# Reading the moving operand's columns alternately from its two halves in both products of a feed-forward stage

## The chip, the core and the metric

The kernel runs on one core of a Trainium2 chip. The metric is device time in microseconds (us), the median over several executions. One further execution was recorded by the hardware profiler; every row quoted below is from that one.

## The reference: what is computed

```python
def _attn_ref(q, k, v, alpha):                # B, H, S, D = 4, 8, 768, 48
    state = np.zeros((B, H, D, D))
    for t in range(S):
        state = alpha[:, :, t, :, None] * state + np.einsum('bhd,bhe->bhde', k[:, :, t], v[:, :, t])
        y[:, :, t] = np.einsum('bhd,bhde->bhe', q[:, :, t], state)

def _moe_ref(x, w_in, w_out):                 # x: 3072 x 384, w_in: 384 x 2048, w_out: 2048 x 384
    h = x @ w_in
    g = np.where(h > 0.0, h, np.exp(np.minimum(h, 0.0)) - 1.0)
    return g @ w_out
```

A gated linear attention over 4 batches, 8 heads and 768 positions gives 3072 rows of 384 numbers. A feed-forward stage (FFN) with an ELU between its two products turns these into the output of 3072 x 384.

## The kernel before, in words

**Attention.** The sequence is cut into 24 windows of 128 positions (6 per batch). A window's operands are loaded on SyncE's queue. VectorE (DVE in the rows) scans the decays, ScalarE (ACT) takes logarithm and exponential, VectorE and GpSimd (POOL) scale keys and queries. TensorE (PE) makes scores (lines L337, L353), state updates (L381, L399) and outputs (L460, L465) by small matmuls. The result of two windows becomes one block `xt` of 256 tokens, held with the 384 features on the partitions, as a rounded part and a rest.

**FFN.** Everything there is done in a split form: each operand is a rounded part of the type float32r plus a rest of the same type, and three of the four cross products are added up. There are 12 blocks of 256 tokens and, for each, 8 steps `j` over 256 of the 2048 hidden units.

- `A(b, j)`, line L662: the first product. The weights are stationary (128 x 128) and the tokens move: each matmul reads 256 columns (tokens) of `xt`. Nine matmuls for each of two groups of 128 hidden units, 18 in all, write one tile `h` (128 x 2 x 256) in PSUM. Over the kernel that is 12 x 8 x 18 = 1728 matmuls.
- `RA`, `RB` on ScalarE, `RC` on VectorE: the ELU. `GH` on ScalarE and `GL` on VectorE make `gh` and `gl`, the rounded part and the rest.
- `O(b, j)`, line L713: the second product. Here `gh` or `gl` (128 hidden units x 128 tokens) is stationary and the weights move: each matmul reads 384 columns of a `w` tile. For each of two halves `m` of the tokens there are six matmuls into an accumulator `o` of 128 x 384 in PSUM; 12 x 8 x 12 = 1152 matmuls in all.
- `Z(b)`: ScalarE copies the two accumulators out and a DMA writes 128 output rows each.

All moving operands of these two products are read column after column from one contiguous run of 4-byte elements: 256 tokens (1 KB in each partition) and 384 weights (1.5 KB).

**Order.** The order in which the work stands on each engine is written out by hand: the string `START` up to the fourth block, and then the string `STEADY`, repeated for each further block with shifts. Each entry is one of the steps above with a window, or a block and a step. The tile framework adds the semaphores. Pools rotate: `gh` and `gl` have three buffers each, `xt` two, and PSUM eight banks, all in one pool.

**Start.** After 12 bfloat16 matmuls on a constant that keep TensorE busy, a helper `probe` (L134) issues further matmuls on a constant tile `fr` (128 x 512, float32r), whose results nobody reads: in this order 5 and 4 of 256 contiguous columns, 8 in bfloat16 of 256 columns (on the same constant as the first 12), 4 whose moving operand is one column of `fr` broadcast to 256, 4 of 256 columns on 64 partitions, and 3 of 512 columns. They stand on TensorE ahead of the first window's transposes (L289).

**Another path.** A function `general` holds a slower version for operands out of the usual range; it is behind a flag and is not executed with these inputs.

Of the kernel before, what the change touches and what calls it, by code (L numbers as in the profile page):

```python
# [14 lines left out]
B, H, S, D = 4, 8, 768, 48  # L15
# [5 lines left out]
DM, DF = 384, 2048  # L21
NC = DM // 128
BLK = 256
NBLK = B * S // BLK
NJ = DF // 256
# [63 lines left out]
def gla_elu_ffn(ctx: ExitStack, tc: tile.TileContext, qka, vv, vn, wgt, out):  # L89
    nc = tc.nc  # L90
# [15 lines left out]
    for a in range(2):  # L106
        nc.vector.tensor_copy(out=sel[64 * a:64 * a + 64, a, :, D:64],
                              in_=ident[64 * a:64 * a + 64, 64 * a:64 * a + D].rearrange("p (x c) -> p c x", c=NC))
# [4 lines left out]
    for h0 in (0, 64):  # L113

        nc.gpsimd.affine_select(
            out=mask[h0:h0 + 64, :], in_=mask[h0:h0 + 64, :], pattern=[[1, C]],
# [5 lines left out]
    wz = first.rearrange("p n w -> p (n w)").bitcast(mybir.dt.bfloat16)  # L122
# [6 lines left out]
    fr = const.tile([128, 512], F32R, name="fr")  # L129
    nc.scalar.copy(out=fr, in_=first.rearrange("p n w -> p (n w)")[:, 0:512])  # L130

    def probe(n, w, lhs, rhs, start):
        for _ in range(n):
            nc.tensor.matmul(wp[:, 0:w], lhsT=lhs, rhs=rhs, start=start, stop=True, skip_group_check=True)  # L134

    probe(5, 256, fr[:, 0:128], fr[:, 0:256], True)
    probe(4, 256, fr[:, 0:128], fr[:, 0:256], False)
    probe(4, 256, wz[:, 0:128], wz[:, 0:256], False)
    probe(4, 256, wz[:, 0:128], wz[:, 0:256], True)
    probe(4, 256, fr[:, 0:128], fr[:, 0:1].broadcast_to([128, 256]), False)  # L140
    probe(4, 256, fr[0:64, 0:128], fr[0:64, 0:256], False)
    probe(3, 512, fr[:, 0:128], fr[:, 0:512], False)

    NB = 4

# [411 lines left out]
    raw, wm, wl, ck, wt, spare = {}, {}, {}, {}, {}, []  # L557
# [93 lines left out]
    @tok  # L651
    def A(b, j):
        x = xt[b]
        h = psa.tile([128, 2, BLK], F32, name="h", tag="pa")
        ff[b, j] = dict(h=h)
        for f in range(2):
            k = 0
            t = wgts[2 * j]
            for c in range(NC):
                ws = slice(f * DM + c * 128, f * DM + c * 128 + 128)  # L660
                for wi, xi in ((0, 0), (0, 1), (1, 0)):
                    nc.tensor.matmul(h[:, f, :], lhsT=t[:, wi, ws], rhs=x[:, c, xi, :],  # L662
                                     start=(f == 0 and k == 0), stop=(k == 8), skip_group_check=True)
                    k += 1

# [35 lines left out]
    @tok  # L701
    def O(b, j):
        d = ff.pop((b, j))
        gh, gl = d["gh"], d["gl"]
        if j == 0:
            ops_[b] = [psa.tile([128, 512], F32, name="o", tag="pa") for _ in range(2)]
        for m in range(2):
            o = ops_[b][m]
            ms = slice(m * 128, m * 128 + 128)
            for f in range(2):  # L710
                t = wgts[2 * j + 1]
                for k, (gt, wi) in enumerate(((gh, 0), (gh, 1), (gl, 0))):
                    nc.tensor.matmul(o[:, 0:DM], lhsT=gt[:, f, ms], rhs=t[:, wi, f * DM:f * DM + DM],  # L713
                                     start=(j == 0 and f == 0 and k == 0),
                                     stop=(j == NJ - 1 and f == 1 and k == 2))

# [46 lines left out]
    with tc.manual_schedule():  # L763
        for name, *at in steady():
            TOK[name](*at)
    main.close()
    general(ctx, tc, ident, [t[:, 0] for t in wgts], [t[:, 1] for t in wgts], flag[0], qka, vn, wgt, out)


# [26 lines left out]
def general(ctx, tc, ident, whi, wlo, flag, qka, vn, wgt, out):  # L796

    nc = tc.nc
    WCH = 2 * DM
    good = nc.values_load(flag[0:1, 0:1], min_val=0, max_val=1)  # L800
    with tc.If(good < 1):
        with ExitStack() as st:
# [5 lines left out]
            for f in range(2 * NJ):  # L808
# [4 lines left out]
                m = sb.tile([128, WCH], F32, name="gwm", tag="gwm")  # L813
# [24 lines left out]
            with tc.For_i(0, B) as b:  # L838
                with tc.For_i(0, NP) as n:
# [7 lines left out]
                    for a in range(2):  # L847
                        nc.sync.dma_start(out=vp[:, :, a, 0:D],
                                          in_=vn4[bass.ds(b, 1), :, :, bass.ds(n * 2 + a, 1), :]
# [7 lines left out]
                    for e in range(D):  # L857
# [3 lines left out]
                        for x in range(2):  # L861
                            nc.tensor.matmul(vb[:, x, 0:HS], lhsT=bc.rearrange("p a x -> p (a x)"),
                                             rhs=vt[:, x * HS:(x + 1) * HS], start=True, stop=True)
# [7 lines left out]
                        for x in range(2):  # L871
                            nc.tensor.matmul(yp[:, x, 0:HS], lhsT=pick[:, 64 - e:192 - e],
                                             rhs=sc[:, x * HS:(x + 1) * HS], start=(e == 0), stop=(e == D - 1))
                    ys = sb.tile([128, S], F32, name="gys")
                    nc.vector.tensor_copy(out=ys.rearrange("p (x t) -> p x t", x=2), in_=yp[:, :, 0:HS])
                    nc.sync.dma_start(out=yd[bass.ds(b, 1), bass.ds(n, 1)].rearrange("b n p s -> (b n p) s"), in_=ys)

            with tc.For_i(0, B) as b:
                with tc.For_i(0, S // BLK) as t:
                    xf = sb.tile([128, NC, BLK], F32, name="gxf")  # L880
                    for a in range(2):
                        for c in range(NC):
                            nc.sync.dma_start(
                                out=xf[64 * a:64 * a + D, c],
                                in_=yd[bass.ds(b, 1), c, 64 * a:64 * a + D, bass.ds(t * BLK, BLK)]
                                .rearrange("b p s -> (b p) s"))
                            nc.sync.dma_start(
                                out=xf[64 * a + D:64 * a + 64, c],
                                in_=yd[bass.ds(b, 1), NP - 1, 64 * a:64 * a + D, bass.ds(t * BLK, BLK)]
                                .rearrange("b (p c) s -> c (b p) s", c=NC)[c])  # L890
                    xh = sb.tile([128, NC, BLK], F32R, name="gxh")
                    xl = sb.tile([128, NC, BLK], F32R, name="gxl")
                    nc.vector.tensor_copy(out=xh, in_=xf)
                    nc.vector.tensor_tensor(out=xl, in0=xf, in1=xh.bitcast(F32), op=ALU.subtract)
                    op = [ps.tile([128, 512], F32, name=f"go{m}", tag=f"go{m}") for m in range(2)]
                    for f in range(2 * NJ):
                        h = ps.tile([128, BLK], F32, name="gh")
                        k = 0
                        fi, fo, f0 = f - f % 2, f - f % 2 + 1, f % 2 * DM
                        for c in range(NC):  # L900
                            ws = slice(f0 + c * 128, f0 + c * 128 + 128)
                            for wt, xt in ((whi[fi], xh), (whi[fi], xl), (wlo[fi], xh)):
                                nc.tensor.matmul(h, lhsT=wt[:, ws], rhs=xt[:, c], start=(k == 0), stop=(k == 8))
                                k += 1
                        r = sb.tile([128, BLK], F32, name="gr", tag="gr", bufs=2)
                        nc.scalar.activation(out=r, in_=h, func=AF.Relu, scale=-1.0)
                        nc.scalar.activation(out=r, in_=r, func=AF.Exp, scale=-1.0)
                        nc.vector.scalar_tensor_tensor(out=r, in0=r, scalar=-1.0, in1=h, op0=ALU.add, op1=ALU.max)
                        gh = sb.tile([128, BLK], F32R, name="ggh", tag="ggh", bufs=2)
                        gl = sb.tile([128, BLK], F32R, name="ggl", tag="ggl", bufs=2)  # L910
                        nc.vector.tensor_copy(out=gh, in_=r)
                        nc.vector.tensor_tensor(out=gl, in0=r, in1=gh.bitcast(F32), op=ALU.subtract)
                        ws = slice(f0, f0 + DM)
                        for m in range(2):
                            ms = slice(m * 128, m * 128 + 128)
                            for k, (gt, wt) in enumerate(((gh, whi[fo]), (gh, wlo[fo]), (gl, whi[fo]))):
                                nc.tensor.matmul(op[m][:, 0:DM], lhsT=gt[:, ms], rhs=wt[:, ws],
                                                 start=(f == 0 and k == 0), stop=(f == 2 * NJ - 1 and k == 2))
                    for m in range(2):
                        ot = sb.tile([128, DM], F32, name="got", tag="got", bufs=2)  # L920
                        nc.scalar.copy(out=ot, in_=op[m][:, 0:DM])
                        nc.sync.dma_start(out=out[bass.ds(b * S + t * BLK + m * 128, 128), :], in_=ot)


# [50 lines left out]
```

## Time and profile before

| | |
|---|---|
| median of 3 executions | 508.41 us (507.92 to 510.58) |
| the profiled execution's own time | 507.37 us |
| its span, first to last instruction | 505.7 us |
| TensorE busy (matmuls) | 495.8 us, 98% |
| TensorE weight loads busy | 480.1 us, 95% |
| VectorE busy | 391.2 us, 77% |
| ScalarE busy | 289.6 us, 57% |
| GpSimd busy | 129.2 us, 26% |
| mean granted TensorE clock | 0.998 of full speed |

The first figure to read is TensorE's busy share, and then the chain of waits, which says whether TensorE's work is what the end waited for. A caution on the duration of a matmul: a matmul of 256 columns lasts 282 ns by its row, but the next one starts long before it ends. What a matmul costs in a dense stretch is the distance from one start to the next; a row of the chain that merges many matmuls gives it, as its time divided by its count.

### The profile page before, as it was taken

Reading aid. Unit: us, or ns where it says so; the run is one execution under the profiler, and the core shown is the slowest. Engines: PE = TensorE matmul, PEld = TensorE weight load, DVE = VectorE, ACT = ScalarE, POOL = GpSimd, SP = SyncE. Lnnn points to the kernel's source line nnn. Section 1 sums busy time; section 2 is a strip of 40 time slices with the busy share of each in tenths; the row PEclk is TensorE's granted clock in tenths of the full one; section 3 lists DMA queues with packets and bytes.
Section 4 is the critical chain, followed back from the end, with each engine's and each line's share of the span. In section 5 each row is a group of like instructions: output and inputs, shape, how many; then the busy total and the mean of one; then the engine's idle time right before and its main releaser. Section 6 shows DMA issues by size and latency. Waiting matters only on the chain.

```text
span 505.7 us, 13302 instructions
## 1 busy us (share of the span) xinstructions
PE 495.8 (98%) x5428; PEld 480.1 (95%) x5428; DVE 391.2 (77%) x808; ACT 289.6 (57%) x690; POOL 129.2 (26%) x108
## 2 busy tenths in 40 slices
PE   8899999998999999999999999999999999999996
PEld 5689999998999999999999999999999999999996
DVE  7999999998899679769969969778978987344221
ACT  3655875744652666647755755646755755454432
POOL 2024954633321301501501501501501500000000
PEclk9999999999999999999999999999999999999999
DMA  8997615034503135235235234234333321110001
GB/s 304 416 412 308 190 48 203 1 94 145 143 1 126 35 108 199 55 109 186 67 110 168 85 110 166 85 109 162 95 102 103 95 72 41 62 40 10 2 32 37
DMA packets 22404, 61.15 MB, mean 121 GB/s; under 512 B 2880, under 2 KB 9792, under 8 KB 22336
## 3 DMA queue, kind: packets, MB, share of 16 engines
q1 hardware_dynamic: 22048, 59.83, 35.3%
q8 instruction: 45, 0.74, 0.6%
q10 hardware_dynamic: 288, 0.39, 0.2%
q14 instruction: 23, 0.19, 0.1%
HBM read 53.53 MB, written 4.72 MB: 115 GB/s over the span
## 4 chain that ended last, share of the span: by engine, by line
PE 93%; DVE 2%; DMA 2%; ACT 1%; SPq 1%; issue 0%; DVEq 0%
PE h L662 41%; PE o L713 40%; PE y L465 4%; PE y L460 2%; PE q L381 2%; PE q L337 2%; DMA qka<-in_qka_dram 1%; PE sc L353 1%; PE u L399 1%; DMA xt<-y 1%; PE y L504 1%; DVE wm L594 0%; DVE wm L600 0%; PE tp L289 0%; DVE qka L238 0%
## 5 line engine op out<-in xcount | busy, mean ns | idle before, releaser
L662 PE MATMUL h<-xt,w 128*128 128x256 f32 x1728 | 215.5, 282 | 1.3 <-DMA xt<-y 1.3
L662 PEld LDWEIGHTS h<-xt,w 128*128 128x128 f32 x1728 | 209.6, 188 | 3.3 <-issue 1.6
L713 PE MATMUL o<-w,gh 128*128 128x384 f32 x768 | 199.1, 340 | 0.0
L713 PEld LDWEIGHTS o<-w,gh 128*128 128x128 f32 x768 | 136.9, 188 | 0.8
L713 PE MATMUL o<-w,gl 128*128 128x384 f32 x384 | 129.9, 338 | 0.0
L686 ACT CAST gh<-h 128x512 fp32r<-128x512 f32 x96 | 56.1, 584 | 80.7 <-DVE h L680 41.4
L699 DVE TENSOR_TENSOR gl<-h,gh 128x512 fp32r<-128x512 f32 x96 | 65.9, 687 | 36.5 <-ACT gh L686 35.0
L299 DVE STREAM_TRANSPOSE kn<-qka 32x128 f32<-32x128 f32 x288 | 87.2, 303 | 4.5
L670 ACT ACTIVATE r<-h 128x512 f32<-128x512 f32 x96 | 57.0, 597 | 52.9 <-PE h L662 50.8
L680 DVE SCALAR_TENSOR_TENSOR h<-r,h 128x512 f32<-128x512 f32 x96 | 64.4, 689 | 16.2 <-ACT r L675 15.3
L238 POOL TENSOR_TENSOR qka<-qka,R 128x512 f32<-128x512 f32 x19 | 25.3, 1334 | 189.1 <-DVE gl L699 117.0
L713 PEld LDWEIGHTS o<-w,gl 128*128 128x128 f32 x384 | 72.1, 188 | 0.0
L675 ACT ACTIVATE r<-r 128x512 f32<-128x512 f32 x96 | 59.1, 632 | 0.6
L268 POOL TENSOR_TENSOR st<-qka,P 64x512 f32<-64x512 f32 x36 | 43.6, 1212 | 15.1 <-DVE P L216 13.3
L365 DVE TENSOR_TENSOR st<-q,mask 64x256 f32<-64x256 f32 x72 | 30.4, 422 | 10.8 <-ACT vs L416 9.2
L216 DVE TENSOR_TENSOR_SCAN P<-qka,first 128x516 f32<-128x516 f32 x24 | 30.2, 1263 | 1.6 <-DMA qka<-in_qka_dram 0.8
L243 POOL TENSOR_TENSOR R<-P,R 128x512 f32<-128x512 f32 x20 | 25.9, 1297 | 7.3 <-DVE qka L238 5.9
L225 ACT ACTIVATE R<-P 128x512 f32<-128x512 f32 x24 | 15.2, 634 | 20.7 <-DVE P L216 20.7
L418 DVE TENSOR_TENSOR vs<-vs,q 48x192 f32<-48x192 f32 x30 | 10.5, 349 | 19.1 <-PE q L337 16.9
L518 ACT ACTIVATE y<-y 128x128 fp32r<-128x128 f32 x20 | 5.6, 278 | 29.7 <-PE y L465 27.4
L618 ACT ACTIVATE ck<-ck,lim 128x384 f32<-128x384 f32 x32 | 20.7, 648 | 0.1
L646 POOL TENSOR_TENSOR w<-spare,w 128x768 fp32r<-128x768 f32 x6 | 15.8, 2649 | 18.8 <-DMA vs<-in_vv_dram 13.0
(106 smaller groups left out, 433.8 us busy)
## 6 DMA issues: line engine op xcount, KB each, us to landing
qka<-in_qka_dram SPq DMA_DIRECT2D x22, 770.0 KB, 6.6
raw<-in_wgt_dram SPq DMA_DIRECT2D x16, 768.0 KB, 10.1
ck<-in_wgt_dram SPq DMA_DIRECT2D x32, 384.0 KB, 3.2
vs<-in_vv_dram SPq DMA_DIRECT2D x36, 192.0 KB, 3.8
out_dram<-ot SPq DMA_DIRECT2D x22, 192.0 KB, 2.0
vs<-in_vv_dram SPq DMA_DIRECT2D x6, 384.0 KB, 10.0
xt<-y SPq DMA_DIRECT2D x40, 48.0 KB, 2.3
qka<-in_qka_dram SPq DMA_DIRECT2D x2, 512.0 KB, 6.1
```

Of the source, the lines that this page charges most:

```text
L216: nc.vector.tensor_tensor_scan(out=P.rearrange("p n w -> p (n w)"), data0=t[:, 2 * NP * W:], data1=first.rearrange("p n w -> p (n w)"), in ...
L243: eng(KBV, i).tensor_tensor(out=d["R"], in0=pw(i), in1=d["R"], op=ALU.mult)
L268: eng(SQV, i).tensor_tensor(out=st[r, a], in0=d["q"][r], in1=pw(i)[r], op=ALU.mult)
L299: nc.vector.transpose(out=kn[32 * t:32 * t + 32, :, 32 * g:32 * g + 32], in_=d["kt"][32 * g:32 * g + 32, :, 32 * t:32 * t + 32])
L365: nc.vector.tensor_tensor(out=d["st"][r, a, :, c * C:(c + 1) * C], in0=d["s4"][a][o], in1=mask[o].unsqueeze(1).broadcast_to([64, NP, C]), ...
L662: nc.tensor.matmul(h[:, f, :], lhsT=t[:, wi, ws], rhs=x[:, c, xi, :], start=(f == 0 and k == 0), stop=(k == 8), skip_group_check=True)
L670: nc.scalar.activation(out=r, in_=d["h"], func=AF.Relu, scale=-1.0)
L675: nc.scalar.activation(out=d["r"], in_=d["r"], func=AF.Exp, scale=-1.0)
L680: nc.vector.scalar_tensor_tensor(out=d["h"], in0=d["r"], scalar=-1.0, in1=d["h"], op0=ALU.add, op1=ALU.max)
L686: nc.scalar.copy(out=gh, in_=d["h"])
L699: nc.vector.tensor_tensor(out=gl, in0=d["h"], in1=d["gh"].bitcast(F32), op=ALU.subtract)
L713: nc.tensor.matmul(o[:, 0:DM], lhsT=gt[:, f, ms], rhs=t[:, wi, f * DM:f * DM + DM], start=(j == 0 and f == 0 and k == 0), stop=(j == NJ - ...
```

## The change

Both products keep their numbers of matmuls and their operands; the order in which the moving columns are read is another. In `A`, the 256 tokens are read as token 0, token 128, token 1, token 129, and so on: the access pattern has an inner dimension of 2 with a step of 128 elements (512 bytes) and an outer one of 128 with a step of 1. So the columns of `h`, `gh` and `gl` hold the tokens in that order, and the output rows come out in it; the host puts the rows back. In `O`, the 384 weights are read as column 0, column 192, column 1, and so on (inner step 768 bytes). The host lays out w_out's columns with the even ones in the first half and the odd ones in the second, so that `o` comes out in the natural order. The path `general` gets the same two forms.

The probes at the start are others: 14 matmuls in place of 28, all float32r on `fr`, all read in such alternating forms: 512 and 384 columns from two halves (3 each), 256 columns from four quarters (3) and from eight parts (2), and 512 columns from four quarters (3).

Apart from the probes, the instructions on each engine stand in the same order as before.

```diff
-    probe(5, 256, fr[:, 0:128], fr[:, 0:256], True)
-    probe(4, 256, fr[:, 0:128], fr[:, 0:256], False)
-    probe(4, 256, wz[:, 0:128], wz[:, 0:256], False)
-    probe(4, 256, wz[:, 0:128], wz[:, 0:256], True)
-    probe(4, 256, fr[:, 0:128], fr[:, 0:1].broadcast_to([128, 256]), False)
-    probe(4, 256, fr[0:64, 0:128], fr[0:64, 0:256], False)
-    probe(3, 512, fr[:, 0:128], fr[:, 0:512], False)
+    def cols(n, k):
+        return fr[:, 0:n].rearrange("p (a x) -> p x a", a=k)
+
+    for n, k in ((512, 2), (384, 2), (256, 4), (256, 8), (512, 4)):
+        probe(3 if k < 8 else 2, n, fr[:, 0:128], cols(n, k), True)
...
-                    nc.tensor.matmul(h[:, f, :], lhsT=t[:, wi, ws], rhs=x[:, c, xi, :],
+                    nc.tensor.matmul(h[:, f, :], lhsT=t[:, wi, ws], rhs=x[:, c, xi, :].rearrange("p (a x) -> p x a", a=2),
                                      start=(f == 0 and k == 0), stop=(k == 8), skip_group_check=True)
...
-                    nc.tensor.matmul(o[:, 0:DM], lhsT=gt[:, f, ms], rhs=t[:, wi, f * DM:f * DM + DM],
+                    nc.tensor.matmul(o[:, 0:DM], lhsT=gt[:, f, ms],
+                                     rhs=t[:, wi, f * DM:f * DM + DM].rearrange("p (a x) -> p x a", a=2),
                                      start=(j == 0 and f == 0 and k == 0),
                                      stop=(j == NJ - 1 and f == 1 and k == 2))
...
-    wo = w_out.reshape(NJ, 2, 128, DM).transpose(0, 2, 1, 3).reshape(NJ, 128, 2 * DM)
+    cols = np.arange(DM).reshape(DM // 2, 2).T.reshape(-1)
+    wo = w_out[:, cols].reshape(NJ, 2, 128, DM).transpose(0, 2, 1, 3).reshape(NJ, 128, 2 * DM)
...
-    return r.results[0]["out_0_dram"]
+    return np.ascontiguousarray(r.results[0]["out_0_dram"].reshape(NBLK, 128, 2, DM).transpose(0, 2, 1, 3)
+                                ).reshape(B * S, DM)
```

More of the change, by code (lines that the diff above doesn't have):

```diff
@@ L876, in general @@
                     nc.sync.dma_start(out=yd[bass.ds(b, 1), bass.ds(n, 1)].rearrange("b n p s -> (b n p) s"), in_=ys)
+            out4 = out.rearrange("(t x a) d -> t x a d", a=2, x=128)
             with tc.For_i(0, B) as b:
@@ L916, in general @@
                             for k, (gt, wt) in enumerate(((gh, whi[fo]), (gh, wlo[fo]), (gl, whi[fo]))):
-                                nc.tensor.matmul(op[m][:, 0:DM], lhsT=gt[:, ms], rhs=wt[:, ws],
+                                nc.tensor.matmul(op[m][:, 0:DM], lhsT=gt[:, ms],
+                                                 rhs=wt[:, ws].rearrange("p (a x) -> p x a", a=2),
                                                  start=(f == 0 and k == 0), stop=(f == 2 * NJ - 1 and k == 2))
@@ L921, in general @@
                         nc.scalar.copy(out=ot, in_=op[m][:, 0:DM])
-                        nc.sync.dma_start(out=out[bass.ds(b * S + t * BLK + m * 128, 128), :], in_=ot)
+                        nc.sync.dma_start(out=out4[bass.ds(b * (S // BLK) + t, 1), :, m]
+                                          .rearrange("t x d -> (t x) d"), in_=ot)
 def kernel(**inputs):
```

## The prediction

> **What bounds the kernel now.** I read the page's busy shares first, then its chain of waits, and then the same chain in order of time for the blocks in the middle.
>
> ```profile
> span 505.7 us, 13302 instructions
> PE 495.8 (98%) x5428; PEld 480.1 (95%) x5428; DVE 391.2 (77%) x808; ACT 289.6 (57%) x690; POOL 129.2 (26%) x108
> PEclk9999999999999999999999999999999999999999
> ...
> PE 93%; DVE 2%; DMA 2%; ACT 1%; SPq 1%; issue 0%; DVEq 0%
> PE h L662 41%; PE o L713 40%; PE y L465 4%; PE y L460 2%; PE q L381 2%; PE q L337 2%; DMA qka<-in_qka_dram 1%; PE sc L353 1%; PE u L399 1%; DMA xt<-y 1%; PE y L504 1%; DVE wm L594 0%; DVE wm L600 0%; PE tp L289 0%; DVE qka L238 0%
> ```
>
> The chain that ended last is TensorE for 93% of the span, and 81% of the span are the two products that the change touches, h (L662) and o (L713). The granted clock is full throughout, so no throttling is there to be gained. To see that this holds stage by stage and not only on average, four stretches:
>
> ```profile
> core 0: us, PE busy (x) PEld busy (x) DVE busy (x) ACT busy (x) POOL busy (x), PEclk, DMA share, GB/s
> 50.00:100.00 50.00, 50.00 (x480) 49.36 (x476) 48.12 (x66) 35.98 (x72) 32.86 (x18) 1.00 0.34 112
> 100.00:191.60 91.60, 90.29 (x1090) 87.53 (x1089) 77.17 (x180) 47.21 (x116) 25.69 (x22) 1.00 0.31 95
> 191.60:422.20 230.60, 230.60 (x2561) 226.98 (x2561) 190.58 (x445) 143.56 (x364) 58.78 (x50) 1.00 0.37 114
> 422.20:501.20 79.00, 78.98 (x601) 78.28 (x599) 30.98 (x62) 36.31 (x78) 0.00 (x0) 1.00 0.07 24
> ```
>
> From 191.6 us to the end of the matmuls TensorE has no gap at all, while VectorE is busy 190.58 of 230.60 us (83%). Only in 50 to 100 us is VectorE nearly as full (48.12 of 50). So a cheaper matmul shortens the kernel almost one for one, and a dearer one lengthens it by all of its price. No wait, buffer or DMA is changed by the edit, and the instructions after the probes stand as before on every engine. The whole question is the price of one matmul.
>
> That price is the distance from start to start in a dense stretch, not the duration in the row (the matmuls overlap). The chain gives it, since it merges dense runs:
>
> ```profile
> 268.31 8.50 PE h L662 x72
> ...
> 285.32 8.48 PE o L713 x48
> ```
>
> h: 8.50 us / 72 = 118.1 ns for 256 columns. o: 8.48 / 48 = 176.7 ns for 384 columns. That is 0.461 and 0.460 ns per column: the price goes with the number of columns, so it looks like a rate of streaming, not like a fixed cost per matmul. The two products are 1728 x 118.1 = 204.1 us and 1152 x 176.7 = 203.6 us, together the 81% of the chain.
>
> **The change part by part.** It adds and removes no FFN matmul. What it alters is which address each moving column comes from: two runs taken in turn instead of one run. The trace of before has no such read. What it has is the probes at the start, which vary one thing at a time (five stretches of the timeline, each read on its own: start, time, count):
>
> ```profile
> 6.58 1.11 PE L134 MATMUL wp<-fr 128*128 128x256 f32 x8
> ...
> 7.65 0.93 PE L134 MATMUL wp<-first 128*128 128x256 bf16 x7
> ...
> 8.53 0.50 PE L134 MATMUL wp<-fr 128*128 128x256 f32 x3
> ...
> 8.75 0.94 PE L134 MATMUL wp<-fr 128*128 128x256 f32 x5
> ...
> 9.18 0.52 PE L134 MATMUL wp<-fr 64*128 64x256 f32 x3
> ...
> L134 PE MATMUL wp<-fr x20: 273/282/496, 6.3 to 10.2; 128*128 128x256 f32 x13, 64*128 64x256 f32 x4, 128*128 128x512 f32 x3
> L134 PE MATMUL wp<-first x8: 272/272/283, 7.5 to 8.3; 128*128 128x256 bf16 x8
> ```
>
> From each I take the last matmul's own duration off and divide by the gaps. Contiguous, 4-byte columns: (1.11 - 0.282) / 7 = 118.3 ns, the same as h in the middle of the kernel, so the probe is a fair stand-in for h, and neighbours on other engines are not the cause. Contiguous, 2-byte: (0.93 - 0.272) / 6 = 109.7 ns. One 4-byte column broadcast to 256 (the three from 8.53): (0.50 - 0.273) / 2 = 113.5 ns by the durations and (8.75 - 8.53) / 2 = 110 ns by the starts; rows are rounded to 10 ns, and I take 112. Half the partitions: (0.52 - 0.278) / 2 = 121 ns, no gain.
>
> So with the weights the same, 6.1 ns of h's 118.1 depend on where the moving columns lie, and 8.4 ns on the 4-byte forms as a whole. The row of the L134 group at 2 bytes also has another weight load, so 8.4 is not the moving side's alone.
>
> [...]
>
> - *h, 1728 matmuls.* Bounds of the new price: 109.7 (the 2-byte row, all the excess gone) and, upward, the slow reads under the rivals. I take the broadcast row's 112, the nearest that has 4-byte columns and the same weights at a changed address pattern: 1728 x 6.1 = 10.5 us saved. All gone would be 1728 x 8.4 = 14.5 us.
> - *o, 1152 matmuls.* No probe has 384 columns. Since the price went with the columns, I scale by 1.5: 6.1 x 1.5 = 9.2 ns, 10.6 us. With a fixed saving per matmul it would be 1152 x 6.1 = 7.0 us, and with all excess gone 1152 x 12.6 = 14.5 us.
> - *The part before 100 us.* Two rows of the stretch, first h's and then o's:
>
> ```profile
> 0.00:100.00 100.00, 32.05 (x252) 30.67 (x252) 1.00 0.63 238
> 0.00:100.00 100.00, 23.25 (x127) 22.22 (x128) 1.00 0.63 238
> ```
>
>  252 x 6.1 + 127 x 9.2 = 2.7 us of the saving lie there, and VectorE has 50 - 48.12 = 1.9 us free in the second half of it. I take 1 us back: what is late next there is VectorE. After 100 us the saving of some 1.4 us per block of 38.4 us leaves VectorE at 190.58 / (230.60 - 6 x 1.4) = 86%.
> - *The probes.* 5504 columns at 0.461 ns are 2.5 us, against 4.1 us now (6.27 to 10.42 by the rows below). They hide behind VectorE:
>
> ```profile
> 6.27 1.42 PE L134 MATMUL wp<-fr 128*128 128x256 f32 x9
> ...
> 10.42 0.60 PE L289 MATMUL tp<-ident,qka 128*128 128x128 f32 x4
> 12.29 0.66 PE L289 MATMUL tp<-ident,qka 128*128 128x128 f32 x4 [0.19 <-DVE qka L248]
> ...
> 9.49 0.69 DVE L248 SCALAR_TENSOR_TENSOR qka<-R,qka 128x512 f32<-128x512 f32 x1
> ```
>
>  The first transposes need VectorE's result at 9.49 + 0.69 = 10.18 and the second ones wait for VectorE again at 12.29, so shorter probes gain nothing. If each took twice as long, they would end near 11.3 and make the second transposes some 0.8 us late, without that cover.
> - *The host's layouts* change no transfer: same tensors, same sizes, same DMAs. The output rows leave in the same contiguous pieces.
>
> Sum: 10.5 + 10.6 - 1.0 = 20 us. The profiled execution took 507.4 us, its span and 1.7 us around it; 507.4 - 20 = 487.4. The median of the runs is 1.0 us above the profiled one: 488.5 us.
>
> **The rivals.**
>
> *Each column from another place costs a read of its own.* The rows are read at 0.46 ns per column when neighbours in the run follow each other; taken in turn from two runs, no column follows its neighbour. If what is fetched with a column is thrown away before the other run's turn ends, the rate halves or worse. The nearest row for a 4-byte stream at a lower rate is that of the plain float32 products that split the weights:
>
> ```profile
> 28.20 0.65 PE wd L635 x2
> ```
>
>  0.65 / 2 = 325 ns for 384 columns, and so 217 for 256. At these prices h costs 1728 x 99 = 171 us more and o 1152 x 148 = 171 us: 850 us. For it: broadcasting shows that addresses matter at all. Against it: nothing in the trace, since no such read is there. It decides from the first nanosecond above 118.1. The mild form is a stall as large as the broadcast's saving, +6.1 and +9.2 ns: 507.4 + 21 = 528.5, 529.5 against the median.
>
> [...]
>
> *Nothing changes.* The excess over the 2-byte row could be that of the 4-byte weight load, which the edit leaves alone:
>
> ```profile
> L134 PEld LDWEIGHTS wp<-fr x20: 183/188/192, 6.2 to 10.0; 128*128 128x128 f32 x16, 64*128 64x128 f32 x4
> L134 PEld LDWEIGHTS <-first x8: 95/98/99, 7.5 to 8.2; 128*128 128x128 bf16 x8
> ```
>
>  188 ns against 98, one per matmul. Then h and o keep 118.1 and 176.7, and the time is 508.4. Against it: the broadcast matmuls have that same load and are 6 ns faster, and o, with the same load under a longer stream, has more excess than h and not less. The other way to nothing is a reader that fetches columns one by one and is blind to their order.
>
> *Only one product gains.* The steps differ (512 and 768 bytes). One product alone gives about 498; this is inside the forecast's own range.
>
> **How the numbers follow.** Faster, with one or both products: 0.54 (488.5 with both; own range 476 to 503, the lower end a little under 508.4 - 29 for all excess gone). Nothing changes: 0.19, 508.4. Mild loss: 0.10, near 529. A read of its own for each column: 0.17, 600 to 850. [...] The range from 476 to 530 leaves out the heavy loss and little else, about 2 in 10. A measurement of this kernel can tell about 0.5% from no change, some 2.5 us; faster is 0.54, same 0.19 and slower 0.27 by the same cases.
>
> **What would show it.** In the profile after, the chain's merged rows of h and o: 8.1 us for 72 and 8.0 us for 48 if I am right; 8.5 and 8.5 if nothing changes; 15 us and more in the heavy rival. If only one row falls, the step of the other one is at fault. The page's PE share should stay at 97 to 98%, with VectorE at 79 to 81%; if TensorE instead shows gaps that VectorE ends, the gain is lost to VectorE's work. The weight load's 188 ns should stay. I am wrong if the spacing of h does not fall below 116 ns, and in the sign if it rises.

## The result

489.41 us median (489.1 to 489.81) against 508.18 us for the kernel before: a ratio of 0.962, with a 95% interval of 0.959 to 0.965. The forecast was 488.5 us. The profiled execution has a span of 487.7 us against 505.7 us.

From the page of the changed kernel (its lines are two lower, L660 for L662 and L711 for L713), the busy shares, the chain of waits and the groups of the two products:

```profile
span 487.7 us, 13274 instructions
PE 472.3 (97%) x5414; PEld 453.0 (93%) x5414; DVE 393.5 (81%) x808; ACT 295.9 (61%) x690; POOL 128.4 (26%) x108
PEclk9999999999999999999999999999999999999998
...
PE 79%; DVE 10%; DMA 3%; issue 3%; ACT 2%; POOL 1%; SPq 1%; DVEq 0%; ACTq 0%; POOLq 0%
...
L660 PE MATMUL h<-xt,w 128*128 128x256 f32 x1728 | 205.7, 277 | 1.8 <-DMA xt<-y 1.8
L711 PE MATMUL o<-w,gh 128*128 128x384 f32 x768 | 188.7, 328 | 0.0
```

TensorE's share of the chain fell from 93% to 79% and VectorE's rose from 2% to 10%: TensorE is still busy nearly all the time, but no longer sets the pace everywhere. The chain in order of time gives the prices; as in the prediction, the price of a matmul is its spacing, the distance from its start to the next one's in a dense stretch:

```profile
205.60 7.80 PE o L711 x48
213.40 2.01 PE h L660 x18
...
262.33 8.41 PE h L660 x72
```

o is now 7.80 / 48 = 162.5 ns (176.7 before) and h 2.01 / 18 = 111.7 ns (118.1). The longer run of 72 takes 8.41 and not the 8.04 that 72 such spacings are: it has waits in it, of which more below. By these prices the matmuls give 1728 x 6.4 + 1152 x 14.2 = 11.1 + 16.4 = 27.4 us; the span shows 18.0. (The expectations below say 11.4, 16.2 and 27.6, from the means of all starts of the two traces.) So there were two questions: why the new order of reading is cheaper, and where the other 9 us went.

### The profile page after: what moved, and what is told of

The parts are those of the page before. It is cut to its first block, busy times and chain, and to the rows that moved or that the text cites. A ratio compares the mean times of both kernels' runs of the same rounds, so it can differ in the third digit from the quotient of the medians.

```text
span 487.7 us, 13274 instructions
## 1 busy us (share of the span) xinstructions
PE 472.3 (97%) x5414; PEld 453.0 (93%) x5414; DVE 393.5 (81%) x808; ACT 295.9 (61%) x690; POOL 128.4 (26%) x108
## 4 chain that ended last, share of the span: by engine, by line
PE 79%; DVE 10%; DMA 3%; issue 3%; ACT 2%; POOL 1%; SPq 1%; DVEq 0%; ACTq 0%; POOLq 0%
PE h L660 35%; PE o L711 34%; PE y L463 4%; PE q L379 2%; DVE kn L297 2%; PE y L458 1%; PE q L335 1%; DMA vs<-in_vv_dram 1%; DMA qka<-in_qka_dram 1%; DVE P L214 1%; DVE gl L697 1%; DVE h L678 1%; DMA xt<-y 1%; POOL w L644 1%; DVE spare L598 0%
## 5 line engine op out<-in xcount | busy, mean ns | idle before, releaser
L660 PE MATMUL h<-xt,w 128*128 128x256 f32 x1728 | 205.7, 277 | 1.8 <-DMA xt<-y 1.8
L660 PEld LDWEIGHTS h<-xt,w 128*128 128x128 f32 x1728 | 199.3, 192 | 5.5 <-issue 3.3
L711 PE MATMUL o<-w,gh 128*128 128x384 f32 x768 | 188.7, 328 | 0.0
L711 PEld LDWEIGHTS o<-w,gh 128*128 128x128 f32 x768 | 132.4, 189 | 1.0 <-ACT gh L684 0.2
L711 PE MATMUL o<-w,gl 128*128 128x384 f32 x384 | 125.8, 328 | 0.8 <-DVE gl L697 0.7
L711 PEld LDWEIGHTS o<-w,gl 128*128 128x128 f32 x384 | 72.5, 189 | 2.0 <-DVE gl L697 1.4
L616 ACT ACTIVATE ck<-ck,lim 128x384 f32<-128x384 f32 x32 | 24.7, 771 | 0.1
L611 ACT ACTIVATE ck<-ck 128x384 f32<-128x384 f32 x32 | 21.9, 683 | 1.8 <-DMA ck<-in_wgt_dram 1.8
L644 POOL TENSOR_TENSOR w<-spare,w 128x768 fp32r<-128x768 f32 x6 | 16.4, 2745 | 19.2 <-DMA vs<-in_vv_dram 13.0
L246 DVE SCALAR_TENSOR_TENSOR qka<-R,qka 128x512 f32<-128x512 f32 x24 | 19.0, 793 | 0.6 <-POOL R L241 0.4
## 6 DMA issues: line engine op xcount, KB each, us to landing
vs<-in_vv_dram SPq DMA_DIRECT2D x6, 384.0 KB, 10.5
```

## The experiments

**1. Which orders of reading are slow.** Two kernels put other matmuls at the start of the changed one, seven of each form (twelve of the first). Nothing reads their results; only their spacings are of interest, not the time of the two kernels (502.59 and 500.73 us, one run each). The edits are abridged.

```diff
+    probe(12, 256, L, fr[:, 0:256], True)            # L: 128 stationary columns
+    probe(7, n, L, fr[:, 0:n], True)                 # n = 256, 384, 512: one run, and
+    probe(7, n, L, cols(n, 2), True)                 # from two halves
+    probe(7, 256, L, near(d), True)                  # pairs d = 2, 4, ... 64 columns apart
+    probe(7, 256, L, runs(r), True)                  # r = 2, 4, 8 columns from each half in turn
+    probe(7, 256, L, fr[:, 0:512:2], True)           # every second column
+    probe(7, 256, L, cols(256, 4), True)             # from four quarters
```

> The changed kernel with other matmuls at the start, whose results nobody reads: seven of each form in turn, all with the same 128 stationary columns, 4-byte moving columns. Read is the distance from start to start of each form. Theory 'lines' (a column from another place than the last costs more the farther it is): two parts cost at least as much as one run at any width, a step of 2 elements costs more than none, and near pairs (2 or 4 elements apart) cost less than far ones. Theory 'one run is the slow case' (a single contiguous run of 4-byte columns loses about one beat in eleven, two interleaved runs lose none): 256, 384 and 512 contiguous columns take 118, 177 and about 225 ns, from two halves 112, 162.5 and 216; the distance between the two columns of a pair can matter, and pairs that lie near each other (2 elements) come out like one run, 118. Runs of 2, 4 and 8 columns from each half in turn should be near 112 if it is only a matter of two sources, and near 118 if the change of place must come at each column. Four parts: 136 again, as in the changed kernel's own probes.

The timeline of that kernel, each stretch read on its own (start, time, count), in the order of the edit. The spacings in the table are means over the seven starts of a form. From a row they come out to within 4 ns as (time - 163 ns) / 7: the row's time is six spacings and the last matmul's own duration, and that is the spacing plus some 163 ns (282 ns at 118.1 in the kernel before; 326 at 162.5 and 380 at 216.5 in the changed kernel's own probes).

```profile
8.03 0.94 PE L134 MATMUL wp<-fr 128*128 128x256 f32 x7
...
8.81 1.39 PE L134 MATMUL wp<-fr 128*128 128x384 f32 x7
10.04 1.30 PE L134 MATMUL wp<-fr 128*128 128x384 f32 x7
11.17 1.79 PE L134 MATMUL wp<-fr 128*128 128x512 f32 x7
12.80 1.67 PE L134 MATMUL wp<-fr 128*128 128x512 f32 x7
...
14.31 1.00 PE L134 MATMUL wp<-fr 128*128 128x256 f32 x7
15.15 0.94 PE L134 MATMUL wp<-fr 128*128 128x256 f32 x7
18.28 0.94 PE L134 MATMUL wp<-fr 128*128 128x256 f32 x7
...
19.06 1.35 PE L134 MATMUL wp<-fr 128*128 128x256 f32 x7
20.24 1.07 PE L134 MATMUL wp<-fr 128*128 128x256 f32 x7
21.15 1.02 PE L134 MATMUL wp<-fr 128*128 128x256 f32 x7
22.01 1.77 PE L134 MATMUL wp<-fr 128*128 128x256 f32 x7
23.59 1.18 PE L134 MATMUL wp<-fr 128*128 128x256 f32 x7
```

| moving columns | spacing, ns |
|---|---|
| 256 / 384 / 512 in one run | 118 / 176 / 234 |
| 256 / 384 / 512 from two halves | 112 / 162 / 216 |
| 256, pairs 2 columns (8 bytes) apart | 120 |
| 256, pairs 4, 8, 16, 32, 64 columns apart | 112 each |
| 256, from two halves in runs of 2 / 4 / 8 | 169 / 130 / 123 |
| 256, every second column | 226 |
| 256, from four quarters | 146 (137 in the changed kernel's own three) |

(118 is the row of before.) The theory that one run is the slow case holds: two interleaved sources cost less than one run at all three widths (112, 162 and 216 ns against 118, 176 and 234), and at 256 columns it makes no difference whether they are 16 or 512 bytes apart (112 each). At 8 bytes the gain is gone (120). What I had not expected are the middle rows: two columns from each half in turn (169) are far worse than either one (112) or all (118), and four sources (146) are worse than one.

The theory that a column from farther away costs more fails: a pair 2 columns apart takes 120 ns, pairs 4 to 64 columns apart and the two halves 112. Every second column of one run, a step of 8 bytes all the way, takes 226. What inside the read path makes it so, these runs do not show.

> The changed kernel with other matmuls at the start, seven of each form, now with the stationary side varied: 64 and 32 stationary columns in place of 128, stationary columns read with a step of 2 and of 4 elements, or one stationary column broadcast. Theory 'the weight load is in the way' (the next weights are read while the moving columns are, and the two get in each other's way when both run through their lines in order): the contiguous 256 columns fall from 118 towards 109.5 with 64 and 32 stationary columns, half and a quarter of the excess left (114 and 111), and stationary columns at another step change the 118 too; 384 contiguous fall from 177 to about 169 and 166. Theory 'the moving read alone': contiguous stays at 118 and 177 whatever the stationary side is. For the two-halves form: if the 111.7 that h now takes is the weight load's own time, it falls to 109.2 with 64 and 32 stationary columns; if not, it stays.

The second kernel varies the stationary side. The rows are 64 stationary columns (256 moving columns in one run and from two halves, 384 in one run); stationary columns at a step of 2 under 256 from two halves; all 128 stationary columns broadcast from one, under 256 in one run; and then the moving column broadcast (256 and 384):

```diff
+            nc.tensor.matmul(wp[0:m, 0:w], lhsT=fr[:, 0:m], rhs=rhs, start=True, stop=True, skip_group_check=True)   # m = 64, 32
+    probe(7, 256, fr[:, 0:256:2], cols(256, 2), True)
+    probe(7, 256, fr[:, 0:1].broadcast_to([128, 128]), fr[:, 0:256], True)
+    probe(7, 384, fr[:, 0:128], fr[:, 0:1].broadcast_to([128, 384]), True)
```

```profile
7.88 0.97 PE L143 MATMUL wp<-fr 128*64 128x256 f32 x7
8.68 0.93 PE L143 MATMUL wp<-fr 128*64 128x256 f32 x7
9.44 1.38 PE L143 MATMUL wp<-fr 128*64 128x384 f32 x7
...
16.55 1.00 PE L134 MATMUL wp<-fr 128*128 128x256 f32 x7
...
19.87 0.96 PE L134 MATMUL wp<-fr 128*128 128x256 f32 x7
20.66 0.94 PE L134 MATMUL wp<-fr 128*128 128x256 f32 x7
21.45 1.32 PE L134 MATMUL wp<-fr 128*128 128x384 f32 x7
```

From two halves, 64 and 32 stationary columns bring the 256 from 111.7 to 109.0 ns (by the starts; both rows are 0.93 us): what h now has left above that goes with its 128 stationary columns; whether it is their load is not shown. One run still takes 115 ns with 64 stationary columns (117 with 32; 118 with 128) and 174 for 384 moving columns (176 with 128), so most of what it takes above the 109 stays with fewer stationary columns. It is not the moving read's alone, though: with all 128 stationary columns broadcast from one, the same run of 256 takes 113.8 ns: nearly half of the 9 ns between 118 and 109 goes with where the stationary columns lie. With 128 stationary columns read at a step of 2, the two-halves form is back at 118.5 (by the starts). So the two reads are not independent, and how they meet stays open. And the moving column broadcast takes 111.8 ns at 256, but 165 ns at 384, 12 below one run. That row would have priced o; more on this in the next section.

**2. One product at a time.** `h_only` leaves the second product's order as before, `o_only` the first one's.

```diff
-                    nc.tensor.matmul(o[:, 0:DM], lhsT=gt[:, f, ms],
-                                     rhs=t[:, wi, f * DM:f * DM + DM].rearrange("p (a x) -> p x a", a=2),
+                    nc.tensor.matmul(o[:, 0:DM], lhsT=gt[:, f, ms], rhs=t[:, wi, f * DM:f * DM + DM],
```

> Only the first product reads alternately. h falls from 118.4 to 111.8 ns, 1728 times, 11.4 us of matmul. If the price of a matmul passes on one for one: 11 us less than before, 497 us. If what is saved before 190 us is mostly taken by VectorE (2.4 of 3.7 us pass) and four fifths afterwards (6.2 of 7.7): 8.6 us less, 499.6 us.

> Only the second product reads alternately. o falls from 176.8 to 162.7 ns, 1152 times, 16.2 us of matmul. If it passes one for one: 492 us. If before 190 us only some 2.4 of 4.9 us pass and four fifths of 11.3 us afterwards: 11.5 us less, 496.6 us. With h alone the two then add up to some 20 us where both together gave 18 to 19, because the same slack at the start is used up by either; if the parts add up exactly, no common limit is at work.

Measured: 500.31 us (ratio 0.985, 0.983 to 0.988) and 495.13 us (0.973, 0.972 to 0.975), 7.9 and 13.1 us less than the kernel before, where the matmuls alone give 11.1 and 16.4. Together 21 us, and both changes in one kernel gave 18.8. Each gain is cut. That the two together are 2 us more than both changes in one kernel fits a common limit, but it is no more than the uncertainty of the three ratios.

**3. Where the gain stops.** One marker in both traces is the run of 72 h matmuls that opens the fifth block. Up to it there are 559 h and 348 o by these rows of the kernel before (stretches of L662 and of L713), worth 559 x 6.4 + 348 x 14.2 = 8.5 us; after it the rest, worth 18.9 us:

```profile
0.00:191.60 191.60, 71.11 (x559) 68.45 (x560) 1.00 0.48 170
0.00:191.60 191.60, 65.31 (x348) 60.52 (x348) 1.00 0.48 170
```

The marker and the last matmul in the timeline of the kernel before, and then of the changed one:

```profile
191.42 8.67 PE L662 MATMUL h<-xt,w 128*128 128x256 f32 x72
...
500.85 0.34 PE L713 MATMUL o<-w,gl 128*128 128x384 f32 x1
```

```profile
189.21 8.47 PE L660 MATMUL h<-xt,w 128*128 128x256 f32 x72
...
482.25 0.33 PE L711 MATMUL o<-w,gl 128*128 128x384 f32 x1
```

Up to the marker 2.2 us are saved of 8.5; behind it 309.43 - 293.04 = 16.4 of 18.9. The stretches of the changed kernel show who is full there:

```profile
50.00:100.00 50.00, 47.94 (x483) 46.58 (x479) 49.49 (x60) 36.06 (x72) 32.84 (x17) 1.00 0.34 112
100.00:189.20 89.20, 85.81 (x1088) 82.48 (x1087) 78.19 (x187) 47.74 (x116) 25.82 (x23) 1.00 0.30 92
189.20:406.00 216.80, 216.80 (x2534) 211.67 (x2535) 188.28 (x439) 148.37 (x366) 58.46 (x50) 1.00 0.39 122
```

TensorE has gaps in the first two, and VectorE is busy 49.49 of 50 us in the first. To test that it is VectorE, and not the order or transfers, four of its steps were left out in both kernels (two of the splitting of the weights, the last one of the key scaling and the state difference); the output is then not the reference's, and only the time is of use:

```diff
     def DB(p):                  # also DC, KC and UB
+        return
```

> The kernel before with four VectorE steps left out (the second and third step of the splitting of the weights, DB and DC, 8 times each; the last step of the key scaling, KC, 24 times; the state difference UB, 18 times): some 60 us of VectorE's 391, and no other engine's work. The output is not the reference's. Bound by TensorE: 508 us less at most a few us at the start, where VectorE is in the chain: 503 to 508.

> The changed kernel with the same four VectorE steps left out. Theory 'VectorE took the rest of the gain': the difference to the kernel before with the same steps left out grows from 18.7 us to about 25 (of 27.6 us of matmul time that the change saves). Theory 'elsewhere': the difference stays at 18 to 19 us.

Measured: 507.91 us and 481.53 us. The kernel before does not care about 56 us less VectorE work (a ratio of 1.000 to the full one, 0.998 to 1.002), the changed one gains 7.9 us by it, and the difference grows from 18.8 to 26.4 us, nearly all of what the matmuls give. Marker and last matmul of the two:

```profile
193.39 8.62 PE L666 MATMUL h<-xt,w 128*128 128x256 f32 x72
...
502.69 0.34 PE L717 MATMUL o<-w,gl 128*128 128x384 f32 x1
```

```profile
184.58 8.20 PE L664 MATMUL h<-xt,w 128*128 128x256 f32 x72
...
474.94 0.33 PE L715 MATMUL o<-w,gl 128*128 128x384 f32 x1
```

Behind the marker 309.30 - 290.36 = 18.9 us: the full price. Up to it the two differ by 8.8 us, but some 2 of these go with the clock and not with the change. In this execution of the kernel before with its steps left out the granted clock was 0.83 between 20 and 30 us, against 1.00 in the full kernel before:

```profile
20.00:30.00 10.00, 8.59 (x144) 7.40 (x145) 6.36 (x10) 6.03 (x18) 0.71 (x1) 0.83 1.02 412
20.00:30.00 10.00, 9.28 (x175) 7.56 (x174) 9.23 (x13) 7.28 (x21) 0.15 (x1) 1.00 1.02 414
```

Its first h matmul starts at 33.35 us, against 31.26, and the distance stays to the marker (193.39 against 191.42). Measured from the full kernel before, 191.42 - 184.58 = 6.8 of the 8.5 us are there. The runs of 72 are now without their waits; in the chain each takes 72 spacings of 111.7 ns:

```profile
256.99 8.04 PE h L664 x72
```

In the changed kernel's chain the eight runs of 72 from the marker on took 8.46, 8.38, 8.41, 8.46, 8.38, 8.42, 8.26 and 8.04 us. Against eight of 8.04 that is 2.5 us: the whole loss behind the marker lies in these runs, although TensorE's busy share there is 100% up to 406 us. Matmuls overlap (an h matmul lasts 277 ns by its row and the next starts 111.7 ns after it), and so the share does not show such waits. Leaving out only the two steps of the weights' splitting, which all lie before the marker, parts the two losses:

> The changed kernel with only the second and third step of the splitting of the weights left out (DB and DC, 16 instructions, 28 to 32 us of VectorE, all before 120 us); the output is not the reference's. The steady part keeps all of VectorE's work. If the loss has two parts, some 6 us before 190 us by VectorE's load there and some 3 us afterwards: the first part alone comes back, 483 us. If the later loss is only an echo of the first: 481.5 us as with all four steps left out. If the weights' splitting is not the load that matters: 489 us.

```profile
184.59 8.47 PE L662 MATMUL h<-xt,w 128*128 128x256 f32 x72
...
477.64 0.33 PE L713 MATMUL o<-w,gl 128*128 128x384 f32 x1
```

485.28 us, where 483 had been expected. The marker comes as early as with all four steps left out (184.59; there the granted clock was 0.83 between 110 and 120 us, which may have cost some of the lead), and the rest takes 293.05 us, as in the full kernel (293.04). So these are two losses, and the second is not an echo of the first. In the steady part it is 2.5 us, and all of it comes back when VectorE's other two steps are left out as well: 293.05 - 290.36 = 2.7. Up to the marker it is 6.3 us by the prices. Of these 189.21 - 184.59 = 4.6 come back, 0.5 of them before the first h matmul already (31.78 against 31.28 us); so some 4 us are VectorE's, and some 2 us stay open.

Two things these runs do not part. A step that is left out takes away its load on VectorE and its place in the chain of waits as well. And GpSimd was busy some 9 us less without the four steps, with the same 108 instructions (120.1 us against 129.2 in the kernel before, 119.7 against 128.4 in the changed one), so part of what came back may have come through it.

**4. Attempts to get it back.** Five kernels move work from VectorE to other engines and leave none out.

```diff
-... KC.6 ... TB.6 O.1.4 ... XH.4 TA.6 GH.0.6
+... KC.6 ... O.1.4 ... XH.4 TP.6 KN.6 GH.0.6        # windows 6 to 11
-WLV, KAV, KBV, SQV = (6, 11, 14), (0, 1, 2, 3, 4), (0, 1, 2, 3), (0, 1, 3)
+WLV, KAV, KBV, SQV = (), (0, 1, 2, 3), (0, 1, 2, 3), (0, 1, 3)      # v_pool
-WPE, XPE, GPE, UPE = (0, 2), (0, 1), (), (1,)
+WPE, XPE, GPE, UPE = (0, 2), (0, 1, 2, 3, 4, 5, 6, 7), (), (1,)      # v_rest; v_both has both
-XL.3 ...
+XP.3 XL.3 ...                                       # v_rest, windows 2 to 7
```

> The kernel before, with the key transposes of windows 6 to 11 made by TensorE (4 matmuls, 0.44 us a window) and a copy on ScalarE, as windows 0 to 5 have it, in place of 16 VectorE instructions (4.8 us a window, 29 us in all between 100 and 190 us). If TensorE alone sets the pace of the kernel before, it becomes slower by TensorE's 2.6 us: 510.8 us. If VectorE already held it up there, it becomes faster.

> The changed kernel with the same move of six windows' transposes from VectorE to TensorE. Theory 'VectorE took the rest of the gain before 190 us' (some 6 us of 8.6 lost there): TensorE's 2.6 us come on, up to 6 us come back, 486 us, and the same move that costs the kernel before is a gain here. Theory 'the gain went elsewhere' (the order of the work, transfers, PSUM): slower by 2.6 us, 492 us.

514.8 us and 495.33 us, ratios of 1.015 and 0.975 to the kernel before: the move costs some 6 us in either kernel, where 2.6 were expected and a gain in the changed one. In this stretch of the changed kernel with the move

```profile
100.00:191.00 91.00, 84.98 (x983) 81.99 (x982) 49.92 (x92) 49.70 (x118) 25.75 (x22) 0.98 0.29 88
```

VectorE is down to 49.92 of 91 us, as meant, and TensorE has more gaps than without the move (6.0 us against 3.4; the granted clock was 0.98 in this stretch and 1.00 in that one). From the same kernel's waits of TensorE between 90 and 200 us:

```profile
PE tp L287 <- DVE st L363: 1.5, 1, 1.5
PE q L335 <- DVE gl L697: 1.3, 2, 1.0
PE q L379 <- ACT kn L316: 1.2, 1, 1.2
```

The transposes now stand in TensorE's queue and wait there for VectorE, 1.5 us in which TensorE is idle, and the state update waits 1.2 us for ScalarE's copy. That suggests that it is not VectorE's load alone that counts, but when a given result comes; it is read from the waits, and no run changes only that.

> The changed kernel with four VectorE instructions of the start moved to GpSimd: the rests of three weight tiles (WL 6, 11 and 14, some 0.95 us each on VectorE, 2.7 on GpSimd) and one product of the key scaling (KA 4, 0.7 us). VectorE has 3.6 us less between 40 and 110 us, where it is full. If VectorE's load there is what holds TensorE up: up to 3 us less, 486.5 us. If GpSimd, slower and sharing with VectorE, becomes the late one, or latency matters more than load: the same or slower, 489 to 493 us.

> The changed kernel with the rests of windows 2 to 7 (XL) formed by TensorE and copied by ScalarE, as windows 0 and 1 have it, in place of VectorE's subtraction: VectorE loses 2 x 0.55 + 4 x 0.83 = 4.4 us between 40 and 150 us, TensorE gets 6 x 0.17 + 4 x 0.06 = 1.3 us and ScalarE some 4 us. If VectorE's load decides: up to 3 us less net, 486.5 us. If the longer chain through three engines decides, as with the transposes moved to TensorE: 490 to 495 us.

> Both moves together: VectorE has 8 us less up to 150 us. If load decides: 484 to 486 us, of the 6 us lost there. If latency or GpSimd decide: no better than the better one of the two alone.

492.9, 490.87 and 493.52 us: none is better than the changed kernel's 489.41, where 484 to 487 was the forecast if load alone decided. With the work on GpSimd the kernel is 3.5 us slower. Why is not shown: the marker is at 192.58 us, 3.4 later than in the changed kernel, but in this execution the granted clock was also 0.57 from 16 to 20 us and again from 74 to 78 us, against 1.00 there (0.992 on the mean against 0.997). GpSimd's price also depends on what runs beside it: in the kernel before its product for `R` (L243) takes 1.20 us in the median of 20, and 2.59 us at 87.26 us beside VectorE's L594, which itself takes 2.25 us there against 1.755 in the median. Forming the rests on TensorE and ScalarE costs some 1.5 us.

## Why the prediction was right, and where it was not

- *What bounds the kernel:* right for the kernel before, as leaving out 56 us of VectorE's work without effect shows. But the step from there, "a cheaper matmul shortens the kernel almost one for one", failed. I gave 1 us back to VectorE. Of the 27.4 us 8.6 were lost, and 7.9 of these came back when four of VectorE's steps were left out. The row for it was quoted, 48.12 of 50 us, and I counted VectorE's idle time in one stretch. From 100 to 191.6 us VectorE had 84% in the kernel before (77.17 of 91.60 us), and TensorE came to wait all the same.
- *h:* 112 ns forecast, 111.7 measured; 10.5 us forecast, 11.1 measured. The broadcast row was the right stand-in, partly by luck: at 384 columns the broadcast (165) and the two halves (162) differ, and at 256 both come out at 112. With 64 stationary columns the two-halves read is at 109.
- *o:* mis-sized. The saving was scaled from h, 6.1 x 1.5 = 9.2 ns; it was 14.2 (16.4 us against 10.6). A row that another limit may hold cannot be scaled: of the two-halves form's 112 at 256 columns, 2.7 ns go with the 128 stationary columns (111.7 against 109.0), and at 384 columns from two halves their number makes no difference (162.2 ns with 128, 162.3 with 64, by the starts). The same broadcast at 384 columns is at 165 ns, a saving of 12. My upper bound, 12.6 ns with all the excess gone, was 1.6 too low.
- *The sum:* 20 us forecast, 18.8 measured, by two errors of opposite sign: 6.3 us more from the matmuls, and 7.6 us more lost than the 1 us taken for VectorE. That 488.5 came so near to 489.41 is luck in this part. A slip beside it changes little: the saving of a block by the prediction's own prices is 21.1 / 12 = 1.8 us and not 1.4, and VectorE's share after 100 us then 87% and not 86%.
- *The probes:* 2.5 us were forecast for them. They took 3.4 (14 of them from 6.82 to 10.22 us), in part because those from four and eight parts of 256 columns are slow (137 and some 210 ns). That they hide behind VectorE was right: TensorE was idle for 0.59 us between them and the first transposes. These start 0.4 us later than before (10.80 against 10.42), because VectorE's work on the first window started 0.5 us later, when its transfer had landed (8.08 against 7.56).
- *The rival of a read for each column:* not for two sources (112 ns where it had 217). Its 0.17, and the 0.27 for a slower kernel with it, were the author's estimate; in no run were single columns from two sources 16 bytes or more apart dearer than one run. Prices of its size do stand nearby: every second column at 226 ns, eight parts at some 210 in the changed kernel's own probes (217 was the rival's).
- *The rival that nothing changes, by the weight load:* refuted by the result itself, since h and o fell (118.1 to 111.7 and 176.7 to 162.5 ns) with the load's duration as it was (188 ns before, 192 and 189 after); and with a half or a quarter of the stationary columns one run still takes 115 to 117 ns.
- *What would show it:* the spacings fell as said in the rows of 18 and 36 h matmuls and of 48 o. The row named for h, that of 72, did not come at 8.1 us but at 8.38 to 8.46, nearer to the 8.5 of no change: its waits, some 0.4 us in each of the first six, are what was lost behind the marker. VectorE's share came to 81% and the weight load's duration stayed (192 and 189 ns). I had also named TensorE gaps that VectorE ends as the sign of a lost gain. The gaps came, but between 33 and 189 us only 0.7 us of them are put down to VectorE, 2.7 to "issue" and 1.8 to a transfer (1.3 in the kernel before). With VectorE's four steps left out only the transfer's is left (1.9); that shows whose most of them were.

## What to carry to other kernels

A dense stream of 4-byte moving columns is worth measuring in more than one order of reading: two interleaved sources took 112 ns for 256 columns at 16 to 512 bytes apart, and 162 and 216 ns for 384 and 512 from two halves, where one run took 6% to 9% more (118, 176 and 234 ns), and every other order of distinct columns that was tried at 256 was no better than one run or far worse (120 to 226 ns). When the engine that bounds a kernel gets cheaper by 5%, look for the stretch in which another engine is as full, and expect the gain to stop there: none of the five kernels that moved work off it won anything back, and only leaving the work out did. And do not scale a price from a row that another limit may be holding.

## What the runs showed of the hardware that was not expected

The order of the moving read has sharp edges: pairs 8 bytes apart 120 ns, 16 bytes apart 112; single columns from two halves 112, two columns from each in turn 169, eight 123; four sources 146. The stationary side has the same kind of edge: read at a step of 2 it makes the two-halves form as slow as one run (118.5 ns), at a step of 4 the one-run form takes 236 ns, and broadcast from one column it makes one run faster (113.8 ns). A TensorE that is busy 100% by its row can still lose time to waits: the changed kernel's first six runs of 72 from the marker on took 8.38 to 8.46 us, and 8.04 without VectorE's four steps.
